# Three small moves of queued work in a one-core attention and expert kernel: a split of ScalarE's transfer requests, a score product set between two groups of turned weights, and a new share of the last stores

## The chip, the cores and the metric

The kernel runs on one core of one Trainium2 chip. The metric is the device time of one execution in microseconds (us). Every time is the median of several executions; a separate execution was taken with the hardware profiler, and all durations of single instructions come from that one.

## The reference

Keys and values are averaged over groups of 8 rows, every head attends to the 72 averaged keys, and the result goes through a two-layer feed-forward part with a periodic activation. All data is float32.

```python
# B = 8 batches, H = 8 heads, S = 576 rows, D = 64, pool = 8, so Sp = 72
k_p = k.reshape(B, H, Sp, pool, D).mean(axis=3)
v_p = v.reshape(B, H, Sp, pool, D).mean(axis=3)
scores = scale * np.matmul(q, k_p.transpose(0, 1, 3, 2))
scores = scores - np.max(scores, axis=-1, keepdims=True)
attn = np.exp(scores)
attn = attn / (np.sum(attn, axis=-1, keepdims=True) + 1e-09)
x = np.matmul(attn, v_p)             # then (B, H, S, D) -> (4608, 512)
h = x @ w_in                         # (4608, 512) @ (512, 2048)
s = np.sin(alpha * h)
g = h + s * s / (alpha + 1e-09)
out = g @ w_out                      # (4608, 2048) @ (2048, 512)
```

## The kernel before

**Stages.** `first_batch` does the attention of batch 0 with nothing beside it. Then nine units of 512 rows go through the first layer (`hidden`), and the attention of the following batch is worked off beside each of them. At the end eight units of 576 rows go through the second layer (`outputs`). Both layers use a fast matrix scheme with 7 instead of 8 block products, so TensorE's products are mixed with additions on VectorE (DVE) and copies on ScalarE (ACT).

**Order.** It is written out by hand: each engine works off its own queue in the order in which the Python code issues, and waits at semaphores alone. `hidden` has 28 slots in a unit: four column groups J of seven products each. In every slot three things are issued in this order: what the slot before left over (`left0` to `left6`: copies, sines, squares, additions), the extras that `carry` entered for this slot with `at(slot, function, ...)`, and then this slot's product (L794). `left0` (L820) copies the bank of a group's first product into the bank on which its third product adds, so that third product waits for L820. `left5` and `left6` issue the group's sines (L800), and later slots its squares (L807).

**The first unit.** Unit 0 carries the attention of batch 1. In slots 13 to 19 `turn` transposes the probabilities on DVE into the buffer `tr`. `move` (L503) then copies `tr` to `aM` with other partitions: for each of 4 blocks there are 2 halves `s` with 2 pieces `c`, that is 16 transfers of 88 to 92 KB. Unit 0 issues blocks 0 to 2 on SyncE (SP) in slot 19, and block 3, four transfers, on ScalarE in slot 20. In the other units SP issues all of them. In slot 23 `a_rest` (L473, L474) transposes the last probabilities of batch 0; ScalarE copies them (`last_t`, L475), and in slot 24 `values_rest` (L575, L577) multiplies them. `all_values` (L592, L605) in slot 26 reads `aM`.

**The start.** In `first_batch`, `products_head(hp)` (L406) makes the scores of head pair hp, `soft_shift` (L412, L414) and `soft_exp` (L420) turn them into exponentials, and `a_head(0, ...)` turns the weights of the first two pairs: two groups of four transposes (L460), each copied by ScalarE (L462), and then four transposes of the remaining keys (L466), copied at L467. `values` (L548, L550) multiplies by v and needs these copies. L519 writes the result as x, for which the first product of unit 0 waits.

**The end.** `out` transposes a finished block on DVE (L1151) and stores it with four transfers (L1156). The last block goes in two parts through one buffer: `early` stores blocks of rows 5 to 8 (four transfers of 32 KB), and `combine` then rows 0 to 4 (four of 40 KB).

**Completion counters.** The program has eight semaphores for the transfers of SP and ScalarE together. Every transfer adds to one of them when it has landed. A later transfer that is given the same one waits, on the queue that issues it, until the earlier transfer has landed. Which one a transfer gets is set when the program is built, in the order of the whole program.

Of the kernel before, what the change touches and what calls it, by code (L numbers as in the profile page):

```python
# [40 lines left out]
class Kernel:  # L41
# [201 lines left out]
    def attention(self, b):  # L243

        nc, D, H, Sp, NP, S = self.nc, self.D, self.H, self.Sp, self.NP, self.S
# [205 lines left out]
            x = self.aM[:].rearrange("p a x -> p (a x)")[:, 0:5 * S].rearrange("p (h n) -> p h n", h=5)  # L451
            return x[:, 0:4], x[:, 4]

        def a_head(g, banks):

            aM, aR = a0_views()
            for e in range(2):
                ps = self.psum([P, 4, P], banks[e])
                for t in range(4):
                    nc.tensor.transpose(ps[:, t, :], self.a0[:, t, 2 * g + e].rearrange("p s k -> p (s k)"), self.ident[:])  # L460
                cp = nc.vector.tensor_copy if g and e else nc.scalar.copy
                cp(out=aM[:, 2 * g + e, 0:4 * P], in_=ps.rearrange("k t n -> k (t n)"))  # L462
            ps = self.psum([P, 4, P], banks[2])
            w = 64 * g + 64
            for t in range(4):
                nc.tensor.transpose(ps[:w, t, :], self.z0[:, t].rearrange("p hp x k -> p (hp x k)")[:, 0:w], self.ident[:])  # L466
            nc.scalar.copy(out=aR[w - 64:w, 0:4 * P], in_=ps[w - 64:w].rearrange("k t n -> k (t n)"))  # L467
# [25 lines left out]
                    nc.vector.transpose(out=tr[:, 0, s, 704:736].rearrange("p (d h k) -> p d h k", d=2, h=2),  # L493
                                        in_=x[:, s, 4:6, 64:Sp].unsqueeze(1).to_broadcast([P, 2, 2, Sp - 64]))

        def move(blocks, queue=nc.sync):

            tr = self.tr[:, 0:2944].rearrange("p (c s x) -> p c s x", c=2, s=2)
            for a in blocks:
                for s in range(2):  # L500
                    for c in range(2):
                        r, w = 64 * s + 32 * c, 704 if c else 736
                        queue.dma_start(out=self.aM[r:r + 32, a, 0:w], in_=tr[32 * a:32 * a + 32, c, s, 0:w])  # L503
# [379 lines left out]
    def first_batch(self):  # L883

        nc = self.nc
        self.att = [self.attention(b) for b in range(self.B)]
        A = self.att[0]

        far = [self.home(i, [P, 4 * POOL * self.D]) for i in (1, 2)]
        h = [self.hp.tile([P, 4 * POOL * self.D], F32, name="h") for _ in range(2)]  # L890
        self.k_rows = far[0][:].rearrange("p (h t d) -> p h t d", h=self.H, t=4)
        self.k_sums = far[1][:, 0:1024].rearrange("p (h u d) -> p h u d", h=self.H, u=2)
        self.new_q(0)
        self.load_alpha(self.hp.tile([P, P], F32, name="s", bufs=1)[:])
        self.load_q_heads(0, 0, 2, nc.scalar)
        add_k = [self.load_k_heads(0, nc.sync, nc.vector)]
        add_rest = self.load_k_rest(h[1][:, 576:832], far[1][:, 1024:1152])
        one = self.sm.tile([P, 1], F32, name="one")
        nc.scalar.activation(out=one[:], in_=self.ident[:, 0:1], func=AF.Sqrt)

        def fill(n):

            for _ in range(n):
                nc.tensor.matmul(self.psum([P, 4, P], 4), self.full[:], self.full[:].unsqueeze(1).to_broadcast([P, 4, P]), start=True, stop=True)
        fill(5)
        self.turn_alpha()
        refine = self.root()
        nc.scalar.activation(out=one[:], in_=one[:], func=AF.Exp)
        add_k[0]()
        tr = self.new_tr()  # L910
        nc.gpsimd.memset(tr[:, 2048:], 0.0)
        self.a0 = tr[:, 0:2048].rearrange("p (t j s k) -> p t j s k", t=4, j=4, s=2)
        self.z0 = tr[:, 2048:2560].rearrange("p (t hp x k) -> p t hp x k", t=4, hp=4, x=4)
        self.kb2 = h[1][:, 0:self.H * self.Sp].rearrange("p (h k) -> p h k", h=self.H)
        self.a4 = self.last[:64, 0:512].rearrange("p (j s k) -> p j s k", j=4, s=2)
        self.z4 = self.last[:64, 512:640].rearrange("p (hp x k) -> p hp x k", hp=4, x=4)
        nc.gpsimd.memset(self.z4, 0.0)
        for hp in range(1, 4):
            add_k.append(self.load_k_heads(hp, nc.sync, nc.vector if hp < 2 else nc.gpsimd))
            self.load_q_heads(0, 2 * hp, 2 * hp + 2)  # L920
        self.load_v_rows(0, h[0][:], self.tp.tile([P, self.DM], F32, name="p5")[:])
        self.load_w_in()
        self.load_w_in_part(0)
        self.q_rest = self.A[3][:64, 0, 512:1024].rearrange("p (h d) -> p h d", h=self.H)
        A.new_a()
        fill(4)
        A.k_head(0)
        add_rest()
        A.q_head(0)
        A.k_last()  # L930
        for f in add_k[1:]:
            f()
        fill(1)
        A.products_head(0)
        A.q_head(1)
        A.k_head(1)
        A.soft_shift(0)
        A.soft_exp(0)
        fill(1)
        A.products_head(1)  # L940
        A.k_head(2)
        A.q_head(2)
        A.soft_shift(1)
        A.soft_exp(1)
        A.norm_head(0, nc.gpsimd)
        A.norm_head(1, nc.vector)
        fill(2)
        A.products_head(2)
        self.sum_v_rest(0, 0)
        self.sum_v_rows(0, 0, 3)  # L950
        A.k_head(3)
        A.q_head(3)
        A.soft_shift(2)
        A.a_head(0, (1, 7, 0))
        self.combine_w_in(0, (0,), nc.gpsimd)
        A.products_head(3)
        A.soft_exp(2)
        A.soft_shift(3)
        A.norm_head(2, nc.gpsimd)
        A.soft_exp(3)  # L960
        A.norm_head(3, nc.gpsimd)
        self.combine_w_in(0, (1,))
        self.combine_w_in(0, (2, 3), nc.gpsimd)
        A.values((0, 1), (5, 6), 2, 0)
        refine()
        self.load_q_rest(0, self.q_rest)
        for e in range(2):
            self.load_k(1, e)
            self.pool_k[e]()
        self.load_q(1)  # L970
        self.load_w_in_part(1)

    def carry(self, u):

        nc = self.nc
# [4 lines left out]
        if u == 0:  # L980
# [33 lines left out]
            for r in (32, 96):  # L1014
                at(3, self.nc.gpsimd.memset, self.aM[r:r + 32, :, 704:736], 0.0)
            at(19, A.move, range(3))
            at(20, A.move, (3,), nc.scalar)
            at(26, A.all_values)
            at(9, self.load_q, 2)
            at(14, self.load_q, 3)  # L1020
# [58 lines left out]
    def outputs(self):  # L1079
# [55 lines left out]
        def early(st):  # L1135

            t = C[st["u"]]["c"]
            with_z(t, st["yz"])
            add(t[:, :, 1], t[:, :, 1], st["x1"][:])
            if st["u"] == self.B - 1:  # L1140
                out(st["u"], 0, 1, t, 5, queues=(nc.sync, nc.scalar))

        def with_z(t, z):
            add(t[:, 1], t[:, 1], z[:, 1:2, :].to_broadcast([P, 2, T]))

        def out(u, i, j, t, n0=0, n1=2 * T // 32, queues=(nc.sync, nc.sync)):

            if n0 or n1 * 32 == 2 * T:
                C[u]["o"] = self.op.tile([P, 2 * T // 32, 2, 32], F32, name="o", bufs=3)
            o = C[u]["o"]  # L1150
            nc.vector.transpose(out=o[:, n0:n1].rearrange("p n h c -> p h n c"),  # L1151
                                in_=t[:].rearrange("p h i c -> p h (i c)").rearrange("p h (n c) -> p h n c", c=32)[:, :, n0:n1])
            r = u * self.S + i * 2 * T
            for a in range(4):
                c = j * 2 * P + a * 64
                queues[a % 2].dma_start(out=self.out[r + 32 * n0:r + 32 * n1, c:c + 64].rearrange("(n k) c -> k n c", k=32),  # L1156
                                        in_=o[32 * a:32 * a + 32, n0:n1].rearrange("k n h c -> k n (h c)"))

        def combine(st):
# [7 lines left out]
            if p in (1, 4, 5):  # L1167

                n = "a" if p == 1 else "b"
                t = c[n] = block("c" + n)  # L1170
                for i in range(2):
                    nc.scalar.copy(out=t[:, :, i], in_=x[i][:])
                with_z(t, z)
                if p == 5:
                    add(c["a"][:], c["a"][:], t[:])
                    out(u, 1, 1, c["a"])
                    add(c["c"][:], c["c"][:], t[:])
            elif p == 2:
                o = block("cd")
                with_x(o, c["a"])  # L1180
                with_z(o, z)
                out(u, 0, 0, o)
            elif p == 6:

                t = c["c"] = block("cc")
                with_x(t, c["a"])
                with_z(t, z)
            elif p == 7:

                t = c["a"]  # L1190
                with_x(t, c["c"])
                with_z(t, z)
                add(c["b"][:], c["b"][:], t[:])
                out(u, 1, 0, c["b"])
            else:
                t = c["c"]
                add(t[:, :, 0], t[:, :, 0], x[0][:])
                if u < self.B - 1:
                    out(u, 0, 1, t)
                else:  # L1200
                    out(u, 0, 1, t, 0, 5, (nc.sync, nc.scalar))

        last = None
        seq = [(u, n) for u in range(self.B) for n in range(7)]
# [177 lines left out]
```

## Time and profile before

| what | value |
|---|---|
| median of 4 executions | 910.91 us (910.15 to 912.93) |
| the profiled execution's own time | 912.0 us |
| span in its profile | 910.2 us |
| TensorE (PE) busy | 899.1 us, 99% of the span |
| weight load (PEld) / VectorE / ScalarE / GpSimd (POOL) busy | 89% / 73% / 48% / 19% |
| granted TensorE clock | 1.00 |

The span is the time from the first to the last instruction in the profile; some 1.8 us of the execution lie around it. A line such as `L503` is a line of the kernel before; after the change the lines below the first edit stand two, three or four further down. PE means the matmuls, PEld the loads of their weights, which run ahead of and beside them. An engine name with a q (`ACTq`, `SPq`) is the engine's sequencer, which issues transfers.

### The profile page before, as it was taken

To read this page: it belongs to the slowest core of one execution; us is meant where nothing else is said; L and a number is where in the kernel's file an instruction comes from. 1 tells how busy PE (TensorE), PEld (TensorE's weight loads), DVE (VectorE), ACT (ScalarE), POOL (GpSimd) and SP (SyncE) were. 2 spreads that over 40 slices of the span, in tenths; PEclk is the share of its full clock that TensorE was granted. 3 is DMA by queue.
4 is the path that set the end of the run, shared out by engine and by line. 5 is a ranking of instruction groups with operands and counts; after the bars stand their busy time and mean duration, and the time that the engine had idled before them with its cause. 6 is when DMAs were issued, how large, how long until landed. Compare 5 with 4: busy or idle time off the path is not lost.

```text
span 910.2 us, 17532 instructions
## 1 busy us (share of the span) xinstructions
PE 899.1 (99%) x6906; PEld 814.3 (89%) x6906; DVE 666.1 (73%) x1000; ACT 436.1 (48%) x998; POOL 171.1 (19%) x159
## 2 busy tenths in 40 slices
PE   8999999999999999999999999999999999999997
PEld 5777888888888788888888899999999999999997
DVE  7675766747667485663466899979888888889895
ACT  5686675867758676686876621121111111111111
POOL 4785250713508044040000000000000000000000
PEclk9999999999999999999999999999999999999999
DMA  9985766768667576538227247161718262533401
GB/s 252 249 245 155 205 180 182 196 177 223 170 185 189 169 196 176 151 107 295 83 90 249 93 115 226 36 219 36 225 27 217 46 184 77 170 92 126 136 15 40
DMA packets 128746, 141.12 MB, mean 155 GB/s; under 512 B 46920, under 2 KB 95704, under 8 KB 128664
## 3 DMA queue, kind: packets, MB, share of 16 engines
q1 hardware_dynamic: 126488, 138.03, 53.1%
q10 hardware_dynamic: 2176, 1.97, 0.8%
q8 instruction: 55, 0.90, 0.4%
q14 instruction: 27, 0.22, 0.1%
HBM read 75.37 MB, written 47.19 MB: 135 GB/s over the span
## 4 chain that ended last, share of the span: by engine, by line
PE 91%; DMA 2%; POOL 2%; SPq 1%; DVE 1%; ACT 1%; issue 0%; ACTq 0%; DVEq 0%; POOLq 0%
PE PS L794 44%; PE PS L1129 42%; PE PS L592 2%; PE PS L302 2%; SPq L659 1%; DMA kvin<-in_v_dram 1%; PE PS L605 1%; DMA a<-in_moe_w_in_dram 1%; DMA h<-in_k_dram 1%; POOL ex L359 1%; POOL kvin L127 0%; POOL as L665 0%; ACTq L503 0%; PE PS L406 0%; SPq L97 0%
## 5 line engine op out<-in xcount | busy, mean ns | idle before, releaser
L794 PE MATMUL PS<-home,a 128*128 128x256 f32 x1152 | 264.4, 381 | 1.9 <-DVE h L773 1.0
L794 PEld LDWEIGHTS PS<-home,a 128*128 128x128 f32 x1152 | 216.5, 190 | 38.3 <-issue 5.0
L794 PE MATMUL PS<-home,as 128*128 128x256 f32 x864 | 200.3, 381 | 0.8 <-ACT PS L820 0.8
L794 PEld LDWEIGHTS PS<-home,as 128*128 128x128 f32 x864 | 162.4, 190 | 24.3 <-issue 1.6
L1129 PE MATMUL PS<-s,wb 128*128 128x144 f32 x896 | 119.3, 286 | 0.4 <-ACT PS L1249 0.4
L1129 PEld LDWEIGHTS PS<-s,wb 128*128 128x128 f32 x896 | 113.7, 190 | 0.7 <-ACT PS L1249 0.6
L127 POOL TENSOR_TENSOR kvin<-kvin 96x768 f32<-96x768 f32 (+3 forms) x42 | 75.9, 1806 | 200.1 <-DMA kvin<-in_v_dram 198.5
L807 ACT ACTIVATE s<-s,c 128x256 f32<-128x256 f32 (+1 forms) x216 | 110.0, 572 | 0.0
L773 DVE TENSOR_TENSOR h<-PS,p 128x512 f32<-128x512 f32 x72 | 49.1, 683 | 78.0 <-PE PS L794 45.6
L800 ACT ACTIVATE s<-h,al 128x256 f32<-128x256 f32 x144 | 65.1, 503 | 56.9 <-DVE h L773 52.7
L1249 ACT COPY PS<-PS 128x144 f32<-128x144 f32 x56 | 14.7, 263 | 145.7 <-PE PS L1129 144.3
L800 ACT ACTIVATE s<-PS,al 128x256 f32<-128x256 f32 x144 | 59.9, 467 | 33.7 <-PE PS L794 18.4
L1129 PE MATMUL PS<-r,wb 128*128 128x144 f32 x512 | 73.2, 286 | 0.0
L1129 PE MATMUL PS<-s,a 128*128 128x144 f32 x512 | 73.2, 286 | 0.0
L865 DVE TENSOR_TENSOR h<-PS,s 128x512 f32<-128x512 f32 x36 | 24.6, 684 | 63.7 <-ACT s L807 63.7
L1129 PEld LDWEIGHTS PS<-r,wb 128*128 128x128 f32 x512 | 67.1, 190 | 0.1
L1129 PEld LDWEIGHTS PS<-s,a 128*128 128x128 f32 x512 | 67.0, 190 | 0.0
L1268 ACT COPY PS<-PS 128x144 f32<-128x144 f32 x56 | 14.7, 263 | 88.5 <-PE PS L1129 88.5
L1129 PE MATMUL PS<-s,we 128*128 128x144 f32 x384 | 54.9, 286 | 0.0
L1129 PE MATMUL PS<-x,wb 128*128 128x144 f32 x384 | 54.9, 286 | 0.0
L865 DVE TENSOR_TENSOR h<-h,s 128x1024 f32<-128x1024 f32 x36 | 51.7, 1435 | 0.0
L1129 PEld LDWEIGHTS PS<-s,we 128*128 128x128 f32 x384 | 50.4, 190 | 0.1
(188 smaller groups left out, 1184.7 us busy)
## 6 DMA issues: line engine op xcount, KB each, us to landing
g_bridge<-h SPq DMA_DIRECT2D x72, 512.0 KB
r<-g_bridge SPq DMA_DIRECT2D x31, 1152.0 KB
out_dram<-o SPq DMA_DIRECT2D x124, 72.0 KB
kvin<-in_k_dram SPq DMA_DIRECT2D x14, 576.0 KB
q<-in_q_dram SPq DMA_DIRECT2D x7, 1024.0 KB
kvin<-in_v_dram SPq DMA_DIRECT2D x14, 512.0 KB
aM<-tr SPq DMA_DIRECT2D x54, 92.0 KB
aM<-tr SPq DMA_DIRECT2D x54, 88.0 KB
```

What stands on the lines that cost most here:

```text
L127: self.nc.gpsimd.tensor_tensor(out=t[..., 0:w] if w > D else out, in0=t[..., 0:w], in1=t[..., w:2 * w], op=OP.add)
L302: nc.tensor.matmul(ps[e][r0 + r:r0 + r + q.shape[-1], h, :], q[s], kb[s, hp, :], start=True, stop=True)
L359: nc.gpsimd.tensor_tensor(out=E(i), in0=E(i), in1=sm.unsqueeze(2).to_broadcast([P, n, Sp]), op=OP.mult)
L592: nc.tensor.matmul(o[r:r + 64], w, x, start=start and i < 2, stop=False, skip_group_check=True)
L773: add = lambda o, x, y: nc.vector.tensor_tensor(out=o, in0=x, in1=y, op=OP.add)
L794: nc.tensor.matmul(ps[:, jj, :], self.A[p][:, kk, f * P:(f + 1) * P], x[:, kk, :], start=(start and jj == 0 and kk == 0), stop=(kk == 1), ...
L800: nc.scalar.activation(out=G.s[:, i, jj, j, :], in_=src[:, jj], func=AF.Sin, scale=self.al[:, f:f + 1])
L807: nc.scalar.activation(out=x, in_=x, func=AF.Square, scale=self.c[:, f:f + 1])
L865: add = lambda o, x, y: self.nc.vector.tensor_tensor(out=o, in0=x, in1=y, op=OP.add)
L1129: nc.tensor.matmul(out, W[:, J // 2, J % 2, :], A[:, J, :], start=(start and J == 0), stop=(J == self.NJ - 1), skip_group_check=True)
L1249: nc.scalar.copy(out=x1[:, 0, :], in_=x0[:, 1, :])
L1268: nc.scalar.copy(out=x1[:, 1, :], in_=x1[:, 0, :])
```

## The change

Three edits, with no instruction added or taken away.

1. `move` takes a list of halves. Unit 0's block 3 is issued in two pairs: half 0 in slot 20 and half 1 in slot 21, both on ScalarE. Between the pairs stand the four sines that `left6` issues at the start of slot 21.
2. `a_head` takes a list of parts. In `first_batch` its two groups of four transposes stand as before, then `products_head(3)` is issued, and then the four transposes of the remaining keys with their copy. Before, `products_head(3)` came after all of `a_head`.
3. `out` takes one queue for each of its four transfers. The last call, for rows 0 to 4 of the last block, uses SP for one and ScalarE for three of them; before, it was two and two. All other calls keep their queues.

```diff
-        def a_head(g, banks):
+        def a_head(g, banks, parts=(0, 1)):
 
             aM, aR = a0_views()
-            for e in range(2):
+            for e in range(2 if 0 in parts else 0):
...
+            if 1 not in parts:
+                return
             ps = self.psum([P, 4, P], banks[2])
...
-        def move(blocks, queue=nc.sync):
+        def move(blocks, queue=nc.sync, halves=(0, 1)):
...
-                for s in range(2):
+                for s in halves:
...
-        A.a_head(0, (1, 7, 0))
+        A.a_head(0, (1, 7, 0), (0,))
         self.combine_w_in(0, (0,), nc.gpsimd)
         A.products_head(3)
+        A.a_head(0, (1, 7, 0), (1,))
         A.soft_exp(2)
...
-            at(20, A.move, (3,), nc.scalar)
+            at(20, A.move, (3,), nc.scalar, (0,))
+            at(21, A.move, (3,), nc.scalar, (1,))
...
-                out(st["u"], 0, 1, t, 5, queues=(nc.sync, nc.scalar))
+                out(st["u"], 0, 1, t, 5, queues=2 * (nc.sync, nc.scalar))
...
-        def out(u, i, j, t, n0=0, n1=2 * T // 32, queues=(nc.sync, nc.sync)):
+        def out(u, i, j, t, n0=0, n1=2 * T // 32, queues=4 * (nc.sync,)):
...
-                queues[a % 2].dma_start(out=self.out[r + 32 * n0:r + 32 * n1, c:c + 64].rearrange("(n k) c -> k n c", k=32),
+                queues[a].dma_start(out=self.out[r + 32 * n0:r + 32 * n1, c:c + 64].rearrange("(n k) c -> k n c", k=32),
...
-                    out(u, 0, 1, t, 0, 5, (nc.sync, nc.scalar))
+                    out(u, 0, 1, t, 0, 5, (nc.sync, nc.scalar, nc.scalar, nc.scalar))
```

## The prediction, made before the changed kernel ran

> **What bounds the kernel now.** The page first: PE is busy for 99% of the span at full clock, so time can only come from a place where PE idles, or from the tail after its last product.
>
> ```profile
> span 910.2 us, 17532 instructions
> PE 899.1 (99%) x6906; PEld 814.3 (89%) x6906; DVE 666.1 (73%) x1000; ACT 436.1 (48%) x998; POOL 171.1 (19%) x159
> ```
>
> Then the waits of PE alone, up to 160 us (total, times, longest):
>
> ```profile
> PE PS L794 <- DVE h L773: 1.0, 1, 1.0
> PE PS L794 <- ACT home L519: 0.8, 1, 0.8
> ...
> PE PS L794 <- ACT PS L820: 0.8, 1, 0.8
> PE PS L575 <- ACT last_t L475: 0.3, 1, 0.3
> ```
>
> Two of the edits each touch one of these: the wait for L519 at 20.67 us (edit 2), and those for L820 and L475 at 75.42 and 77.69 (edit 1). The chain of waits shows what feeds the latter (start, us, what):
>
> ```profile
> 70.19 0.20 DVE tr L493 x2
> 70.39 0.54 ACTq L503
> ...
> 72.51 0.60 ACTq L503
> 73.11 0.05 issue
> 73.16 0.13 ACT s L800
> ...
> 74.79 0.49 ACT PS L820
> 75.28 2.05 ACT s L807 x4
> 77.33 0.32 ACT last_t L475
> 77.64 0.04 issue
> 77.69 0.75 PE PS L575 x16
> ```
>
> ScalarE spends 70.32 to 73.11 issuing four transfers, with no arithmetic. Its four sines, the copy L820, four squares and the copy L475 follow without a gap, and PE waits for the second and the last of these. Last, the timeline of the tail:
>
> ```profile
> 905.36 0.79 SPq L1156 DMA_DIRECT2D out_dram<-o  x2
> 905.36 1.84 ACTq L1156 DMA_DIRECT2D out_dram<-o  x4
> 907.11 0.80 SPq L1156 DMA_DIRECT2D out_dram<-o  x2
> ```
>
> SP's last pair starts at 907.11, although the transpose that makes its data ended at 906.22 and SP was free at 906.15. It waited for a completion counter: ScalarE's first early store landed at 907.05. Its second landed at 907.53, and SP's last store starts at 907.54 and lands at 909.14; the program's closing waits end about 1 us later.
>
> **What the Trainium skill says.** Perfetto Trace Analysis, "DVE / Act Engine Instruction": the sequencer pushes an instruction into a queue and is then free for the next, so it can run ahead of the engine. The same page, "DMA Instruction — HWDGE": a transfer is issued by the sequencer itself, which is busy until the descriptors are made. Together: a request behind queued arithmetic is issued while the arithmetic runs, but arithmetic behind a request waits. The trace agrees. At 523 us one ScalarE request, which stands behind all four squares in the program, is issued during the first of them:
>
> ```profile
> 523.03 0.51 ACT L807 ACTIVATE s<-s,c 128x256 f32<-128x256 f32 x1
> 523.18 0.39 ACTq L1075 DMA_DIRECT2D r<-g_bridge  x1
> 523.43 1.72 ACT L807 ACTIVATE s<-s,c 128x256 f32<-128x256 f32 x3
> ```
>
> DMA: Bandwidth & Descriptors, "Issuing engines are not separate DMA queues": using several issuers saves only issue time. That fits the tail, where landings and not issue set the end.
>
> **Edit 1, the split pair.** The first pair starts at 70.32 as before, since it waits for DVE's transposes, and ends at 71.83 (0.61 and 0.86 us with a gap). Now the sines follow. Their inputs are there: DVE's addition ended at 70.95, and PE's product for the last two at 70.75 (16 matmuls from 68.76 make two products, the first ends there, the second at 72.48). So the four sines start at 71.87 instead of 73.16, 1.29 us earlier, and keep the engine until 73.40 (73.16 to 74.68 before). The sequencer has pushed them by about 72.0 and issues the second pair under them: two at 0.55 and 0.60 with gaps, until 73.2 (73.6 if one takes 0.86). Its counters are free: one waits for SP's first transfer, landed at 72.31. L820 needs PE's product of 72.48, so it starts at 73.4, 1.28 us earlier, and ends at 73.99.
>
> PE can use only part of this. Before its third product stand the product from 72.32 and the five transposes to 74.66. In the weight loads, which show the issue order best, the last transpose's ends at 74.52 and the next stands at 75.39; it can now follow at about 74.53: **0.86 us**. The squares and L475 then end at 76.35 instead of 77.64. PE's weight loads for the third product, 1.59 us from first to last, end at 76.1, and such a change to 64-row weights takes 0.33 us elsewhere in the trace (82.06 to 82.40), so L575 loads at 76.43 instead of 77.69: **1.26 us in all**. By the matmuls' own idle time it is 0.76 + 0.30 = 1.06; ends of matmuls are modelled, so I take 1.2, with 1.0 (slow requests) to 1.3 as bounds.
>
> What is late next? The second pair issues at most 0.1 us later than before and lands by about 75.7. SP's 11th move now shares a counter with it, but SP reaches that at 76.66. `aM` is complete when SP's last move lands at 79.42; `all_values` needs it at 82.40, or 81.2 after the gain. DVE's L865, which waited for the squares, starts 1.3 earlier; the turn of q behind it (80.20) must still wait for the landings and moves by 0.5, and q's last piece lands at 94.6 instead of 95.1, against the scores that need it at 100.07. From there PE has no gap that anything fixed in time holds, so the 1.2 us stay.
>
> **Edit 2, scores between the turned weights.** Nothing is added; 4 transposes and 32 score matmuls change places. The scores need the copy L386, ended at 16.60, and a change of weight rows costs 0.2 us, so they start at about 16.8 instead of 17.22, 0.4 earlier; `soft_shift(3)` on DVE follows. But the four transposes end 0.8 later, at about 18.05, so L467 ends at 18.65 instead of 18.04. With the two changes of row count `values` starts 0.2 to 0.3 later, and L550 would start at 18.97 instead of 18.74 and end at 20.09 instead of 19.86. L519 now starts when L550 ends, 20.13, no longer after `soft_exp(3)`: 20.26 before. So PE gains 0.1 at 20.67, with −0.3 (transitions cost more) to 0.4 (none) as bounds. And whatever the sign, it is taken back: at 68.76 PE's weight load stands 0.22 us behind the one before, for DVE's L773, which is behind the `turn` of block 2. That goes back through POOL's chain, unbroken from 46.4 us, to the landing of v at 46.35, a transfer that SP issued behind a landing. A gain stops there; a loss of up to 0.2 does too. **0.0**, bounds −0.1 to +0.1 on the end.
>
> **Edit 3, the last stores.** SP issues three of the eight and ScalarE five. Counters move with them. SP's second early store now waits for ScalarE's first early store (907.05), so it starts at 907.09 instead of 905.72. SP's only last store waits for ScalarE's second (907.53) and starts at 907.58, where its last one started at 907.54. ScalarE's third last store follows at 907.25 (0.45 us of issue) and lands after 1.7 us like its others, at 908.95. The end is again a store issued at 907.5 to 907.6: landing at 909.15, **0.0**, bounds −0.1 (the counter frees sooner, since one store less is ahead) and +0.4.
>
> **Sum.** −1.2 + 0 + 0: the span falls from 910.2 to 909.0, the profiled execution from 912.0 to 910.8. That execution lies 1.1 above the median, and the span alone 0.7 below it; the difference is carried over to the median: 910.91 − 1.2 = **909.7**.
>
> **The rivals.**
> - *The second pair doesn't hide.* If it were issued only after the sines have run, it would take 73.4 to 74.6, and L820 would start at 74.68 as before. For it: SP issues beside it, and one request of the first pair took 0.86. Against it: the lines at 523 us. Time: 910.9.
> - *Edit 2's gain isn't taken back.* If the landing of v, or POOL's work, comes earlier with a different overlap of DVE and POOL, part of the 0.81 at 20.67 or of the 1.02 at 56.21 goes too. For it: DVE's L865 of 47.17 lasts 2.76 us beside POOL against 1.21 alone, so small shifts can change durations. Against it: 68.76. Time: 910.9 − 1.2 − 0.8 = 908.9.
> - *The tail grows, slower.* Three stores (32, 40, 40 KB) instead of two are now issued from 907.09 on. In the last phase landings follow each other by 0.2 to 0.5 us (907.95, 908.44, 908.65, 909.14); one more ahead of the last puts it at 909.55, +0.4. It decides only if edit 1 gives less than that, as in the first rival: 911.3.
>
> **The numbers.** Main forecast 0.60, not hidden 0.15, edit 2 passes 0.17, slower tail with no gain 0.08. Differences under 0.2% (1.8 us) are about what a measurement of this kernel can tell from no change: its four executions spread over 2.8 us. The main case lies 0.6 inside that bound and crosses it in about a fifth of cases, by the scatter of two medians; edit 2's case crosses it in most. Faster 0.29, same 0.64, slower 0.07. The range 908.6 to 911.1 takes in the main case with its scatter, most of the second rival and the unhidden pair. The main case alone is 909.2 to 910.2.
>
> **What would show it.** In the timeline of ScalarE: sines at 71.9, requests issued under them, L820 at 73.4. In PE's waits: the lines for L820 and L475 gone, the one for L519 near 0.7, a wait at 68.76 unchanged. In the tail: SP's stores at 907.1 and 907.6 less 1.2 us. Wrong: L820 still at 74.7, or `all_values` waiting for a transfer, or a last landing more than 1.6 us after SP's last issue.

## The result, and the profile after

The changed kernel takes **909.47 us** (median of 43 executions, 907.85 to 911.97) against 910.71 us (63 executions) in the same measurement: ratio 0.9987, 95% interval 0.9982 to 0.9991, that is 0.8 to 1.6 us less. The forecast was 909.7.

The head of the page after:

```profile
span 907.4 us, 17532 instructions
PE 899.0 (99%) x6906; PEld 814.8 (90%) x6906; DVE 664.7 (73%) x1000; ACT 436.4 (48%) x998; POOL 170.0 (19%) x159
```

The waits of PE up to 160 us (total, times, longest), to be held against the eight lines of before, of which the prediction shows four:

```profile
PE PS L906 <- DVE full L1284: 1.1, 1, 1.1
PE PS L796 <- DVE h L775: 0.7, 1, 0.7
PE PS L796 <- ACT home L521: 0.5, 1, 0.5
PE PS L406 <- ACT q L386: 0.2, 1, 0.2
PE PS L406 <- ACT h L369: 0.2, 1, 0.2
```

The lines for L820 and L475 (now L822 and L477) are gone, and those for L519 (L521) and L773 (L775) are smaller. A wait of 0.8 us at L374 is gone too; it lies at 7 us, ahead of all that the edits touch, and in the other profiles it lasts 0.3 to 0.6 us or is missing. The timeline of ScalarE shows how the lines for L820 and L475 went, at the place of the split (start, us, engine, line, what; the idle time before it in brackets):

```profile
69.27 1.50 ACTq L505 DMA_DIRECT2D aM<-tr  x2
70.82 0.51 ACT L802 ACTIVATE s<-h,al 128x256 f32<-128x256 f32 x1 [2.21 <-DVE h L775]
70.93 0.52 ACTq L505 DMA_DIRECT2D aM<-tr  x1
71.23 0.49 ACT L802 ACTIVATE s<-h,al 128x256 f32<-128x256 f32 x1
71.61 0.51 ACTq L505 DMA_DIRECT2D aM<-tr  x1
71.63 0.82 ACT L802 ACTIVATE s<-PS,al 128x256 f32<-128x256 f32 x2
72.34 0.59 ACT L822 COPY PS<-PS 128x512 f32<-128x512 f32 x1
```

The third request (70.93 to 71.45) lies under the first two sines, the fourth under the last two. The engine runs sines and copy without a gap.

**The profiles differ by more than the medians.** The profiled execution of after took 909.26 us, that of before 912.0: 2.7 us less (their spans, 2.8), where the medians give 1.2. Comparing PE's weight loads one by one from start to end shows where: 1.05 us are already there when slot 20 begins (68.76 before, 67.71 after), 1.18 come between slot 20 and L575, 0.61 somewhere between there and PE's end, 0.01 in the tail. The second part is edit 1. Where the first comes from is what the experiments had to tell.

### The profile page after: what moved, and what is told of

It reads as the page before. It is cut to its first block, busy times and chain, and to the rows that moved or that the text cites. A ratio compares the mean times of both kernels' runs of the same rounds, so it can differ in the third digit from the quotient of the medians.

```text
span 907.4 us, 17532 instructions
## 1 busy us (share of the span) xinstructions
PE 899.0 (99%) x6906; PEld 814.8 (90%) x6906; DVE 664.7 (73%) x1000; ACT 436.4 (48%) x998; POOL 170.0 (19%) x159
## 4 chain that ended last, share of the span: by engine, by line
PE 98%; DVE 1%; ACT 0%; issue 0%; DVEq 0%; ACTq 0%
PE PS L796 48%; PE PS L1133 42%; PE PS L302 2%; PE PS L594 2%; PE PS L607 1%; PE PS L906 0%; PE PS L406 0%; PE PS L385 0%; PE PS L552 0%; PE PS L274 0%; PE PS L263 0%; PE PS L199 0%; PE PS L550 0%; PE PS L368 0%; DVE cc L1088 0%
## 5 line engine op out<-in xcount | busy, mean ns | idle before, releaser
L127 POOL TENSOR_TENSOR kvin<-kvin 96x768 f32<-96x768 f32 (+3 forms) x42 | 72.5, 1727 | 198.0 <-DMA kvin<-in_v_dram 196.3
L775 DVE TENSOR_TENSOR h<-PS,p 128x512 f32<-128x512 f32 x72 | 49.1, 684 | 77.8 <-PE PS L796 44.7
L802 ACT ACTIVATE s<-h,al 128x256 f32<-128x256 f32 x144 | 65.1, 503 | 54.6 <-DVE h L775 53.9
L802 ACT ACTIVATE s<-PS,al 128x256 f32<-128x256 f32 x144 | 60.0, 467 | 32.2 <-PE PS L796 17.0
L1133 PEld LDWEIGHTS PS<-x,wb 128*128 128x128 f32 x384 | 50.3, 190 | 0.0
```

The source lines that it names most:

```text
L127: self.nc.gpsimd.tensor_tensor(out=t[..., 0:w] if w > D else out, in0=t[..., 0:w], in1=t[..., w:2 * w], op=OP.add)
L775: add = lambda o, x, y: nc.vector.tensor_tensor(out=o, in0=x, in1=y, op=OP.add)
L802: nc.scalar.activation(out=G.s[:, i, jj, j, :], in_=src[:, jj], func=AF.Sin, scale=self.al[:, f:f + 1])
L1133: nc.tensor.matmul(out, W[:, J // 2, J % 2, :], A[:, J, :], start=(start and J == 0), stop=(J == self.NJ - 1), skip_group_check=True)
```

## The experiments

Two times recur in all profiles. **p** is PE's weight load of unit 0's first product (20.67 before), **v** is the start of GpSimd's first addition on batch 1's v, which begins 0.1 us after that load has landed (46.49 before).

**1. Each edit alone.** Edit 1:

```diff
-            at(20, A.move, (3,), nc.scalar)
+            at(20, A.move, (3,), nc.scalar, (0,))
+            at(21, A.move, (3,), nc.scalar, (1,))
```

> Edit 1 alone. Theory (the whole of the change is the pair of requests that hides under the sines): 1.2 us less than before, 1.0 to 1.3, ratio 0.9987; in the trace the four sines end about 1.3 us earlier against the first request than before, and PE waits neither for L820 nor for L475. Rival (edit 2 carries a part of the 1.2 us measured for the whole change): edit 1 alone gives 0.5 to 0.9 us. Rival (noise in two medians): no difference.

Measured: 909.3 us against 910.55, ratio 0.9988 (0.9981 to 0.9995), 1.25 us less. PE waits neither for L820 nor for L475. So edit 1 alone gives as much as the whole change, with an interval of 0.5 to 1.7 us.

Edit 2:

```diff
-        A.a_head(0, (1, 7, 0))
+        A.a_head(0, (1, 7, 0), (0,))
         self.combine_w_in(0, (0,), nc.gpsimd)
         A.products_head(3)
+        A.a_head(0, (1, 7, 0), (1,))
```

> Edit 2 alone. Theory (taken back at the landing of v): 0.0, within 0.1 us of before in the median; PE's wait for L519 falls from 0.8 to 0.4-0.7 us, but PE stands at the products of slot 20 at a time that follows the landing of batch 1's v (22.3 to 22.4 us behind it, as in the run before), whatever the wait was. Rival (it passes): 0.3 to 0.8 us less.

Measured: 910.06 against 910.55, ratio 0.9995 (0.9988 to 1.0003). The interval, 1.1 us less to 0.3 more, doesn't separate the two theories; the trace does for its execution. PE's weight load at slot 20 stands 22.30 us behind v, as in the run before (22.27), and both waits for ScalarE are whole:

```profile
PE PS L796 <- ACT PS L822: 0.8, 1, 0.8
...
PE PS L796 <- ACT home L521: 0.5, 1, 0.5
PE PS L577 <- ACT last_t L477: 0.3, 1, 0.3
```

But the trace holds something that was not in the forecast. Counted from one of PE's weight loads just ahead of the moved ones, p comes 0.06 us earlier with edit 2: 4.80 us behind it in all four profiles with the edit, 4.86 in all ten without it. At the weight load for L263, near 34 us, PE has won another 0.42 us, of which 0.36 are left from the next load on. In the timeline of before, around 31 us, GpSimd adds up k while DVE makes a difference of two inputs:

```profile
31.49 2.46 POOL L127 TENSOR_TENSOR kvin<-kvin 96x384 f32<-96x384 f32 x1
...
31.82 0.67 DVE L767 TENSOR_TENSOR home<-home 128x512 f32<-128x512 f32 x1
32.42 0.68 DVE L767 TENSOR_TENSOR home<-home,home 128x512 f32<-128x512 f32 x1
```

The same three in the timeline of after:

```profile
30.96 1.00 POOL L127 TENSOR_TENSOR kvin<-kvin 96x384 f32<-96x384 f32 x1
...
31.46 1.05 DVE L769 TENSOR_TENSOR home<-home 128x512 f32<-128x512 f32 x1
32.44 1.07 DVE L769 TENSOR_TENSOR home<-home,home 128x512 f32<-128x512 f32 x1
```

With edit 2 GpSimd is 0.50 us ahead instead of 0.33, and now DVE waits for GpSimd rather than GpSimd for DVE. Against p, the sum of k is ready 1.3 us earlier, and PE's weight load for L263 no longer waits for it (a gap of 0.53 us before, 0.11 after). So it is in three of the four profiles with edit 2 (in the fourth GpSimd came to this place 1.2 us later against p and lost again), and in none of the ten without. Edit 2 is thus worth 0.06 + 0.36 = 0.42 us to PE behind this place; whether any of it reaches the end is the question of experiment 3.

Edit 3:

```diff
-                    out(u, 0, 1, t, 0, 5, (nc.sync, nc.scalar))
+                    out(u, 0, 1, t, 0, 5, (nc.sync, nc.scalar, nc.scalar, nc.scalar))
```

> Edit 3 alone. Theory: 0.0 (-0.1 to +0.4 us); SP's second early store starts at the landing of ScalarE's first early one, SP's only last store at the landing of ScalarE's second, and the distance from PE's last product to the end of the span is the same as before within 0.05 us. Rival (the tail grows, since three stores are issued late): 0.4 us more in that distance and in the median.

Measured: 910.54 against 910.55, ratio 1.000 (0.999 to 1.001). SyncE's second early store starts 1.98 us behind PE's end (1.95 by the forecast) and its only last store 2.39 behind it (2.44); from PE's end to the end of the span 5.08 us, as before.

Taken further, all four on ScalarE:

```diff
-                    out(u, 0, 1, t, 0, 5, (nc.sync, nc.scalar))
+                    out(u, 0, 1, t, 0, 5, 4 * (nc.scalar,))
```

> Edit 3 taken further, alone: all four of the last stores on ScalarE, the early ones two on SyncE and two on ScalarE. Theory (the end is set by a store issued about 2.4 us behind PE's last product, whichever queue issues it): SyncE's second early store waits for the landing of ScalarE's second early one and is issued last, beside ScalarE's fourth; from PE's last product to the end of the span 5.0 to 5.25 us (5.08 before). Rival (the queue matters: four issues of 0.45 us in a row on one engine, or more bytes late): 5.4 us or more.

Measured in one profile: 5.08 us again. SyncE's two early stores now both wait for the landings of ScalarE's early ones (timelines of SyncE and of ScalarE, end of this run):

```profile
904.39 0.79 SPq L1156 DMA_DIRECT2D out_dram<-o  x2
```

```profile
903.72 1.86 ACTq L1156 DMA_DIRECT2D out_dram<-o  x4
```

PE ended at 902.55, so the second of SyncE's is again issued about 2.3 us behind it, and its landing comes 4.0 us behind PE's end, as in the kernel before. ScalarE's fourth store is issued later still (905.12) and lands at 4.23 us, but the closing waits on SyncE, which begin when its own store has landed, last until 4.28, and it hides under them. Three different shares give the same end; that the last store sets it on whichever queue, as the theory had it, is not what this run shows.

**2. How many requests stand ahead of the sines.** After two of four, none:

```diff
-            at(20, A.move, (3,), nc.scalar)
+            at(21, A.move, (3,), nc.scalar)
```

> Edit 1 taken further: all four of ScalarE's requests for block 3 stand behind the four sines (slot 21); edits 2 and 3 left out. Theory (what counts is that the sines come first; requests behind pushed arithmetic cost PE nothing): the same as edit 1 alone, 1.2 us less than before, within 0.3 us of edit 1 alone; the four requests are issued in one row of about 2.6 us beside the sines, and the copy L820, which stands behind them in the sequencer, starts within 0.3 us of where it starts with edit 1 alone, since four requests last longer than four sines by about the time by which the sines wait for L773. Rival (L820 is now held by the requests): a wait of PE for L820 of 0.5 us or more comes back, and the gain is half or less.

Measured: 909.17 against 910.38, ratio 0.9987 (0.9980 to 0.9994), 1.21 us less and the same as edit 1 alone. ScalarE's timeline:

```profile
69.54 0.60 ACTq L503 DMA_DIRECT2D aM<-tr  x1
69.64 0.81 ACT L800 ACTIVATE s<-PS,al 128x256 f32<-128x256 f32 x2
70.18 2.05 ACTq L503 DMA_DIRECT2D aM<-tr  x3
72.33 0.57 ACT L820 COPY PS<-PS 128x512 f32<-128x512 f32 x1 [1.88 <-issue]
```

Here the sines end at 70.45, and the copy does stand behind the requests until 72.23; but PE has no wait for it: the copy ends 5.50 us behind PE's weight load of slot 20, and the third product's weights load at 5.94. This profile had the earliest v of all (43.58), for which the table below leaves edit 1 nothing to win, so it is the medians that carry the comparison. Two requests behind the sines or four make no measurable difference, so what edit 1 needs is that the sines come first.

And eight ahead of them:

```diff
-            at(19, A.move, range(3))
-            at(20, A.move, (3,), nc.scalar)
+            at(19, A.move, range(2))
+            at(20, A.move, (2, 3), nc.scalar)
```

> The opposite of edit 1, as a dose: block 2's four transfers join block 3's on ScalarE in slot 20, so eight requests stand ahead of the sines; SyncE keeps blocks 0 and 1. Theory (every request ahead of the sines is paid in full by PE once the wait for L820 is there): four more requests at 0.6 to 0.75 us move the sines and L820 by 2.4 to 3.0 us, PE's wait for L820 is about 3.2 us instead of 0.8, and the time is 2.4 to 3.0 us more than before, minus nothing. Rival (the requests were only seemingly on the path, PE's wait has another cause): 0 to 0.5 us more.

Measured: 915.54 against 910.38, ratio 1.0053 (1.0038 to 1.0068), 5.2 us more: the sign and the path are the theory's, the size is not. The eight take 4.76 us of issue and 1.35 us of gaps, the largest (0.38 and 0.63 us) ahead of the fifth and the seventh, which were given the counters of the first and the third and wait until those have landed. So L820 starts 3.3 us later against the first request than before. The rest is PE itself (timeline of PE, before and in this run; then this run's table by stages, whose last columns are the granted clock, the DMA share and GB/s):

```profile
75.42 1.97 PE L794 MATMUL PS<-home,as 128*128 128x256 f32 x8 [0.76 <-ACT PS L820]
...
78.02 3.50 PE L794 MATMUL PS<-home,as 128*128 128x256 f32 x8 [4.08 <-ACT PS L820]
```

```profile
74.00:78.00 4.00, 0.00 (x0) 0.01 (x1) 0.00 (x0) 2.24 (x6) 3.84 (x4) 0.97 0.83 170
78.00:81.50 3.50, 3.48 (x12) 2.53 (x12) 1.54 (x2) 2.24 (x5) 2.01 (x3) 0.55 0.00 0
81.50:84.00 2.50, 2.50 (x33) 2.18 (x33) 2.50 (x4) 1.55 (x6) 0.00 (x0) 1.00 0.53 198
```

After 4.08 us without work PE ran at 0.55 of its clock for 3.5 us: its weight loads stand 0.427 us apart instead of 0.216, and eight matmuls took 3.50 us instead of 1.97. From slot 20 to L575 this run needs 13.41 us, the kernel before 8.93: 4.5 of the 5.2 us.

**3. When v lands.** The load of v goes ahead of the last four weight transfers (1 MB):

```diff
-            at(2, self.load_w_in_part, 3)
...
             at(7, self.load_v, 1)
+            at(7, self.load_w_in_part, 3)
```

> The kernel before with one other change: in unit 0 the six transfers of batch 1's v are issued ahead of the last four first-layer weight transfers (1 MB) instead of behind them. Theory (the landing of v sets PE's place at slot 20): v lands about 3 us earlier (43.4 instead of 46.35), the wait of 0.2 us at slot 20 goes and so does most of the 1.0 us for L773 at 56.2, where the 2.76 us addition L865 beside GpSimd is passed earlier; 0.3 to 1.2 us less. Rival (PE's own order sets the place, the landing has slack): within 0.1 us of before. Rival (the weights, now later, become the late input): slower, by a wait of PE for L665's sums.

Measured: 909.15 against 910.55, ratio 0.9988 (0.9978 to 0.9997), 1.4 us less (0.3 to 1.2 were expected), with none of the three edits. v begins at 44.16 (a gain of 2.3 in these two profiles, not 3), the gap at slot 20 is gone, and of the waits for L820 and L475 one of 0.2 us is left: the requests start 2.0 us earlier, PE only 1.2. So in this place it is v's landing that makes the requests late.

> Batch 1's v issued ahead of the last four first-layer weights, with edits 1 and 3. In the run with v alone moved, the landing was early enough that the requests began 0.8 us earlier against PE and only 0.2 us of PE's waits for ScalarE was left in that place. Theory (edit 1 and the early landing take away the same wait): 0.2 us less than v alone moved, that is 1.4 to 1.8 us less than before. Rival (independent, they add): 1.4 and 1.2 add up to 2.6 us less than before.

Measured: 909.18 against 910.38, ratio 0.9988 (0.9981 to 0.9994): 1.2 us less (0.5 to 1.7), not 2.6; the theory's 1.4 lies inside the interval. The two gains don't add.

> The whole change (edits 1, 2, 3) with batch 1's v issued ahead of the last four first-layer weights. Theory (edit 2's 0.35 us at 20.3 is taken back only by the landing of v, and with an early landing at most 0.3 us of it passes): 0.2 to 0.35 us less than the same kernel without edit 2, 1.7 to 2.0 us less than before, and no gap in PE's weight loads at slot 20. Rival (the landing of v is not what takes it back): the same time as without edit 2.

Measured: 908.95 against 910.38, ratio 0.9987 (0.9979 to 0.9994): 1.4 us less than before, where 1.7 to 2.0 were expected, and 0.2 less than without edit 2, well inside the scatter of the two medians. This is the lowest median of all, but it isn't told apart from the changed kernel. It is also the profile in which edit 2's gain at L263 did not appear, so what edit 2 is worth with an early v stays open.

The other way, v later: its two large transfers, which GpSimd needs first, behind its four small ones.

```diff
-        for s in range(2):
-            nc.sync.dma_start(out=t[64 * s:64 * s + 64], ...)
         for s in range(2):
             for c in range(2):
                 r = 64 * s + 32 * c
                 nc.sync.dma_start(out=x[r:r + 32], ...)
+        for s in range(2):          # for b == 1 alone
+            nc.sync.dma_start(out=t[64 * s:64 * s + 64], ...)
```

> The kernel before, but batch 1's v is loaded in the other order: its four small transfers first, then the two of 512 KB on which GpSimd's first addition waits; nothing else is moved. Theory (PE's place after slot 20 follows the landing): the first addition on v begins about 1.1 us later than without this (46.5 on the mean of such profiles instead of 45.4), ScalarE's first request for block 3 begins 23.85 us behind it and the weight load of L575 31.2 us behind it, and the time is 0.8 to 1.4 us more than before. Rival (PE's own row of products sets the place, the landing has slack): no difference.

> The same late v, with edit 1. Theory: PE's waits for L820 and L475 are gone, but PE is now held at slot 20 by L773, 22.3 us behind the first addition on v, and the weight load of L575 stands 30.05 us behind it; 1.1 to 1.2 us less than the late v without edit 1, so about as long as before (-0.3 to +0.3 us). Rival (edit 1's gain doesn't depend on v, and the late v is hidden): 1.2 us less than before.

> The same late v, with edits 1 and 2. Theory (edit 2's gain at the first product is swallowed at slot 20 when v is late): the same as the late v with edit 1 within 0.3 us; the wait for L519 is 0.47 instead of 0.81 us, and the gap in PE's weight loads at slot 20 is larger by what was won. Rival (edit 2 passes): 0.35 us less than with edit 1 alone.

Measured, against 910.19: 910.84 (ratio 1.0007, 0.9997 to 1.0017), 910.75 with edit 1 (1.0005, 0.9998 to 1.0013), 910.98 with edits 1 and 2 (1.0011, 1.0001 to 1.0021). The first is 0.65 us more, where 0.8 to 1.4 were expected, and its interval takes in no difference. With a later v neither kernel with edits is faster than before, as the theory has it. The 1.1 us expected between the first two do not show; means of 14 and 13 executions, which spread over 5 and 3 us, leave a difference of 1.1 less to 0.7 more, so this one is missed or at the edge. The profile of the first kernel happened to have an early v (44.45), but the fixed distances hold in it: the request 23.85 and L575 31.23 us behind v. In the other two PE is held at slot 20, but 22.06 and 21.59 us behind v instead of 22.3. With edit 1, and with edits 1 and 2 (timeline of GpSimd, its first addition on v, then of PE; in these kernels L794 stands at L800 and L802):

```profile
47.34 3.02 POOL L127 TENSOR_TENSOR kvin<-kvin 128x1024 f32<-128x1024 f32 x1 [7.30 <-DMA kvin<-in_v_dram]
...
69.41 1.78 PE L800 MATMUL PS<-home,a 128*128 128x256 f32 x7 [1.50 <-DVE h L779]
```

```profile
47.71 2.55 POOL L127 TENSOR_TENSOR kvin<-kvin 128x1024 f32<-128x1024 f32 x1 [8.71 <-DMA kvin<-in_v_dram]
...
69.30 1.99 PE L802 MATMUL PS<-home,a 128*128 128x256 f32 x8 [1.50 <-DVE h L781]
```

PE stands idle for 1.50 us at slot 20 in both. Edit 2's gain was to be lost here, and this idle time to grow by it; it doesn't. Against p, PE begins slot 20 at 48.61 us with edit 2 and at 48.98 without, 0.37 us earlier, although v comes 0.11 us later. The additions show why. In both runs v lands when DVE has begun a long addition (46.92 to 48.14, and 46.82 to 48.03 with edit 2), and GpSimd's own ends 2.23 us behind the end of DVE's; slot 20 stands 19.04 us behind that. So what holds PE here is no longer the landing but DVE's addition, which edit 2 brings 0.36 us forward. At L575, 0.17 us of the gain are left. So it isn't shown that edit 2 gains nothing when v is late; the means of 13 and 14 executions leave anything from 0.6 us less to 1.3 more.

Where edit 2's gain is lost can be read from another pair, edit 2 alone and four stores on ScalarE, with v 24.56 and 24.57 us behind p. PE is 0.36 us ahead with edit 2 at slot 19, 0.25 at slot 20 and 0.04 at L575, where it waits for ScalarE in both. There the requests, which follow v, take it back. In the changed kernel's own profile it is gone at slot 13, at the wait for L775: that slot begins 34.82 us behind p, with edit 2 alone 34.41.

**All profiles together.** Where v is loaded in its old order and ScalarE has two or four requests in slot 20 (request: ScalarE's first for block 3; slot 20 and L575: PE's weight loads):

| profile | v - p | request - v | slot 20 - v | L575 - v |
|---|---|---|---|---|
| before | 25.82 | 23.83 | 22.27 | 31.20 |
| edit 2 alone | 24.56 | 23.86 | 22.30 | 31.23 |
| edit 3 alone | 26.00 | 23.87 | 22.38 | 31.26 |
| four stores on ScalarE | 24.57 | 23.88 | 22.54 | 31.26 |
| edit 1 alone | 24.92 | 23.86 | 22.30 | 30.05 |
| changed kernel | 25.10 | 23.85 | 22.29 | 30.04 |

From v to the request the chain is fixed to 0.05 us in these six programs, and L575 follows it at 31.2 us without edit 1 and at 30.05 with it. The landing itself is what moves: in the eight profiles with v in its old order it lies between 43.6 and 47.1. PE's own row of work would bring L575 at p + 55.0 (54.98 with edit 1 alone, 55.02 with four late requests). So in an execution edit 1 is worth the later of v + 31.2 and p + 55.0, less the later of v + 30.05 and p + 55.0: all of 1.15 us if v - p is over 24.95, nothing under 23.8. Over the six profiles with the old order and without edit 2 (the table's, and 25.49 with eight requests and 23.29 with four late ones) that is 0.9 us on the mean, against the measured 1.2. This is an estimate from single profiles, and p + 55.0 is its weakest part: in the three profiles with v early, L575 stands 55.3 to 55.6 us behind p.

## Why the prediction was right, point by point

**Edit 1: right, step by step.** Counted from the first request, the sines were to start at 1.55 and started at 1.55; the second pair was to be issued by 2.88 and was by 2.85; L820 at 3.08, was 3.07; the third product's weight load at 4.21, was 4.27; L475's end at 6.03, was 6.03; L575's load at 6.11, was 6.19. The gain of 1.18 us in this stage is the 1.2 of the sum. The rival of a second pair that doesn't hide is refuted by the timeline.

**Edit 2: right in the end, wrong on the way.** The scores start 0.4 us earlier, as worked out, and PE gains 0.06 us at its first product (0.1 was said). The wait for L519 fell by 0.34 us, from 0.81 to 0.47, where "near 0.7" was said: most of that is PE's own work ending later, not PE starting earlier. What the sum left out is GpSimd: the 0.36 us won near 34 us are the mechanism that the second rival named (a shift that changes who waits for whom), at another place than the one it named. That the work behind v takes the gain back was right for the changed kernel's profile, at slot 13 already. The step that was too firm is "a gain stops there": it rested on one execution. v - p differs from one to the next, and in the pair with v late the gain passed slot 20. How much of it reaches the median is not shown.

**Edit 3: right.** 0.0, with SyncE's stores within 0.05 us of where they were placed.

**From the profile to the median.** The sum was carried over unchanged from an execution with v at 46.49 to a median over executions of which some have it 2 us earlier. In those edit 1 gains less, and the forecast didn't say so. It held because v was mostly late enough (in five of the six profiles above edit 1 is worth 0.8 us or more), which the prediction had not checked: here it was lucky. For the profiled execution it gave 910.8, and 909.26 was measured. Of the 2.7 us by which the two profiled executions differ, 1.07 is the landing of v (46.49 and 45.42) and 1.18 edit 1. The 0.6 behind L575 is open: PE needs between 826.4 and 827.5 us from there to its end in the fourteen profiles, with and without each edit, and the small waits that make it, in units 3 to 5, were not followed up.

## What to carry to other kernels

Here requests ahead of arithmetic on one queue delayed it by their whole issue time, and the same requests behind the arithmetic cost nothing, since what followed had slack; look for a queue's issue time in the chain ahead of a wait. Before a stall is priced, follow it back to something that is fixed in time: here one input's landing set the waits at three places, and two changes that gained 1.2 and 1.4 us by themselves gained 1.2 together. When a landing scatters by 3.5 us from one profile to the next, a single profile shows one draw of it, so compare distances to the landing rather than times from the start.

## What the runs showed of the hardware that was not expected

- **PE's clock after a pause.** 4.08 us without work were followed by 3.5 us at 0.55 of the clock, and a pause of 1.50 us by none (its next stage was granted 1.00). The Trainium skill, TensorE: Matmul & The Clock Gate, "What's actually happening", says that PE goes to half its clock after an idle window of about 3.4 us and back after a busy one; both durations agree. This stall cost another 1.5 us in the eight matmuls behind it.
- **GpSimd against DVE.** Which of two meeting additions waits changed between two leads 0.17 us apart: with 0.33 us ahead, GpSimd's lasted 2.46 us and DVE's kept 0.67; with 0.50 ahead, it lasted 1.00 and DVE's took 1.05. The Trainium skill, SBUF — State Buffer, "SBUF: two separate sides", says that the two share a port pair, and that of a GpSimd instruction and a DVE one with two inputs in SBUF the one that starts first holds it for its whole instruction. Where DVE had started first, in the late pair above, GpSimd's addition did wait for its end. But by the recorded starts it isn't so at a lead of 0.33 us, where the measurement decides. That GpSimd's first access lies later than its recorded start by more than that would explain it; it wasn't tested.
